# Chunk bounds from a second load of k, q turned in 32x32 blocks: a chunk-selecting attention with a gated FFN on one core

## The chip, the core and the metric

The kernel runs on one core of a Trainium2 chip. The core has TensorE for products (PE in the profile; its weight loads are listed as PEld), VectorE (DVE), ScalarE (ACT), GpSimd (POOL) and SyncE (SP), which here only issues transfers. TensorE writes to PSUM, eight banks; all else is kept in SBUF, 128 partitions wide. The metric is the device time of one execution in microseconds (us).

## The reference

```
def _attn_ref(q, k, v) -> np.ndarray:
    B, H, S, D = q.shape
    chunk = 32
    nc = S // chunk
    top_k = 6
    ...
    k_min = np.min(k_chunks, axis=3)
    k_max = np.max(k_chunks, axis=3)
    ub = np.sum(np.maximum(q[:, :, :, None, :] * k_min[:, :, None, :, :], q[:, :, :, None, :] * k_max[:, :, None, :, :]), axis=-1)
    ...
    ub = np.where(causal, ub, -1000000000.0)
    top_chunks = np.argsort(ub, axis=-1)[..., -top_k:]
    scores = scale * np.matmul(q, k.transpose(0, 1, 3, 2))
    ...
    scores = np.where(mask, scores, -1000000000.0)
    ...
    return np.matmul(attn, v).astype(np.float32)

def _moe_ref(x, w_gate, w_val, w_out, rms_g) -> np.ndarray:
    rms = np.sqrt(np.mean(x * x, axis=-1, keepdims=True) + 1e-06)
    xn = x / rms * rms_g
    g = xn @ w_gate
    silu = g * (1.0 / (1.0 + np.exp(-g)))
    val = xn @ w_val
    return (silu * val @ w_out).astype(np.float32)
```

q, k and v are fp32: batch 4, 8 heads, 768 tokens, 64 channels; the FFN has 3072 tokens, 512 wide, 1536 hidden. The mask holds the chosen chunks and causality, and attn is the softmax of the scores. Attention is causal, and a query attends only to the six chunks of 32 keys whose upper bound `ub` is highest. The result, with the heads side by side, goes through an RMS norm and a gated FFN.

## The kernel before

Work is cut into 16 pairs: a pair is two heads of one batch, and four pairs make a batch. Every piece of work is a step, recorded by `add(name, engines, ...)` with what it depends on and which buffers it opens. The long string `PROGRAM` holds the order: each word names an engine (P, A, D, G for POOL, S), the number of a step and the buffer slots that it opens. `Order.run` emits the steps in that order, and each engine runs its own steps strictly in it. A step waits for those it depends on and for the last users of its slots. The numbers in the `add` calls are what the search for an order was told; nothing in the kernel reads them at run time. `SLOTS` (line 232) says how many buffers of a kind there are.

For a pair, `prep` (line 479) loads q and k as tiles `qnat` and `knat` of 128 tokens by 2 x 64 channels, and TensorE turns each in six fp32 transposes (`turn`, line 514, tiles `pq` and `pk`). ACT or DVE evict them to `qt` and `kt`, channels on partitions (helper `evict`, lines 289 to 295, whose lines stand in the profile for many steps). From `kt`, two reductions per pair give the largest and smallest key of each chunk (`kmx`, and `ku` for the smallest, lines 546 and 548), and `dif` subtracts them. Since max(q x min, q x max) = q x min + relu(q) x (max - min), the bound is a sum of two products: `ku` with `qt`, and the difference with `rt`, which is relu of `qt` (`relu`, line 630). POOL casts `kt` to bf16 halves `ke` (`cast`, line 614), beside which `ke` holds a constant indicator of chunks, `e_all`.

For pairs from number 3 on (`QM`), q reaches its bf16 form `qs` on another way: POOL lays `qnat` out as bf16 in `qn` (`lay`, line 551), the chosen chunks are written beside it (`pick`, line 657), and SP issues two DMA transposes (`turned`, line 555) into `qs`. The same way for k is in the code for pairs from `KSIDE` on, which is 16, so that no pair takes it. For pairs from 6 on (`DUO`), two pairs share one step of bound products (`duo`, line 770): 16 products on tiles of 64 rows by 32 columns with 384 columns each, two evictions to `ubd`, six transposes back (`up`), the causal mask (`ubm`), then eight-largest searches (`top`, line 644) and `pick`, which also writes a guard row from the largest bound.

`scores` (line 843) multiplies `ke` by `qs` into `sc`, ACT takes the exponential into `pt`, POOL masks the diagonal (pairs of batch 1 on), and TensorE multiplies by `vx` into `av`. DVE normalizes into `xb`. `norm` and `ffn` (lines 937, 1017) run per batch and half: gate and val products of four matmuls each (`gp`, `vp`), tanh on ACT, `tg` and `hh` on DVE, each of which frees the PSUM bank of its product, then three times three output steps (`po`). The FFN of one batch is interleaved with the attention of the next ones. The lowest part of the program, until the first gate product of batch 0, has fillers for TensorE (`busy`, line 338).

Of the kernel before, what the change touches and what calls it, by code (L numbers as in the profile page):

```python
# [198 lines left out]
def kernel(  # L199
# [25 lines left out]
    W = S // 2  # L225
    G = 3
    DUO = 6
    KSIDE, QM = 16, 3
    HW = NT * P + D
    NPAIRS = B * NP  # L230

# [247 lines left out]
    def prep(c, i0, nb, at, lr):  # L479
# [85 lines left out]
        if side_k:  # L565
            def red2(e, which, j0, bank):
                a0, a1 = j0 * 4, (j0 + 3) * 4
                if which == 0 and mx.tile is None:
                    tile_of(mx, [P, NCH], FP32, "kmx")
# [580 lines left out]
```

## Time and profile before

| | us |
|---|---|
| median of 3 runs | 314.37 (314.15 to 315.52) |
| the profiled execution | 314.75 |
| its span, first to last instruction | 313.0 |
| busy in the span: PE, DVE, ACT, POOL | 303.2, 231.5, 185.5, 103.9 |

The profile shows one execution. A row of a group has the line, engine and operation, what it writes and reads, the count, the total busy time, the mean of one in ns, and the idle time of its engine just before it. A chain row has the start, the length and the group. Busy times contain an instruction's latency, which overlaps with the next one's start: 96 of the 128x128 transposes of k last 277 ns each and yet take less than half of that on the chain when they follow each other.

### The profile page before, as it was taken

What the parts mean: (1) busy time and instruction counts of PE and PEld (TensorE: products, weight loads), DVE (VectorE), ACT (ScalarE), POOL (GpSimd) and SP (SyncE); (2) the same over time, 40 slices, a digit from 0 to 9 for tenths busy, and PEclk for the clock granted to TensorE, in tenths of its full rate; (3) what the DMA queues carried; (4) which work ended last, traced back from release to release, by engine and by line L of the source; (5) the groups of instructions that cost most, each with busy time, mean ns of one, the idle gap of its engine ahead of it and who ended that gap; (6) DMA issues with size and microseconds to landing.
All of it is one profiled execution on the core that took longest, in us unless ns stands there. A gap on an engine that the chain in (4) does not pass through costs nothing.

```text
span 313.0 us, 7431 instructions
## 1 busy us (share of the span) xinstructions
PE 303.2 (97%) x2772; PEld 191.7 (61%) x2790; DVE 231.5 (74%) x654; ACT 185.5 (59%) x415; POOL 103.9 (33%) x162
## 2 busy tenths in 40 slices
PE   7998999999999999999999999999999999999994
PEld 3676776576576855667687546656666545555541
DVE  4998989969985789856978879989544564577551
ACT  1688998783298773697794643366697403442001
POOL 8686453371354843252377100033233110000000
PEclk9999999999999999999999999999999999999998
DMA  9999999999699996797684060361240034100014
GB/s 173 220 190 126 96 191 206 201 165 168 129 185 198 220 114 146 175 191 138 138 68 28 17 140 13 52 77 36 58 79 36 2 78 155 69 3 0 2 67 169
DMA packets 113301, 35.35 MB, mean 113 GB/s; under 512 B 106225, under 2 KB 110065, under 8 KB 113265
## 3 DMA queue, kind: packets, MB, share of 16 engines
q1 hardware_dynamic: 83152, 26.62, 41.1%
q0 software_dynamic: 28512, 7.87, 24.9%
q10 hardware_dynamic: 1600, 0.39, 0.6%
q8 instruction: 22, 0.36, 0.5%
q14 instruction: 15, 0.11, 0.1%
HBM read 28.57 MB, written 6.29 MB: 111 GB/s over the span
## 4 chain that ended last, share of the span: by engine, by line
PE 87%; DMA 5%; DVE 4%; POOL 1%; issue 1%; SPq 1%; ACT 1%; POOLq 0%
PE po L1078 20%; PE vp L1058 19%; PE gp L1037 19%; PE sc L868 9%; PE av L904 5%; DMA wv<-in_moe_w_val_dram 4%; PE pk L517 3%; PE busy L338 3%; PE pq L517 3%; PE ub L781 2%; PE ub L723 2%; PE up L803 1%; DMA qs<-qn 1%; DVE m L650 1%; DVE qs L293 1%
## 5 line engine op out<-in xcount | busy, mean ns | idle before, releaser
L885 ACT ACTIVATE pt<-sc 128x512 bf16<-128x512 f32 (+2 forms) x192 | 92.9, 561 | 17.5 <-PE sc L868 15.4
L1044 ACT ACTIVATE sg<-gp 128x384 bf16<-128x384 f32 x96 | 45.5, 496 | 55.1 <-PE gp L1037 42.2
L1050 DVE SCALAR_TENSOR_TENSOR tg<-sg,gp 128x384 bf16<-128x384 bf16 x96 | 51.8, 550 | 32.0 <-ACT sg L1044 30.6
L1058 PE MATMUL vp<-xT,wv 128*128 128x384 bf16 x384 | 74.0, 326 | 0.3 <-DMA wv<-in_moe_w_val_dram 0.2
L1037 PE MATMUL gp<-xT,wg 128*128 128x384 bf16 x384 | 73.2, 326 | 0.7 <-ACT xT L289 0.4
L1078 PE MATMUL po<-wo,hh 128*128 128x512 bf16 x272 | 66.9, 379 | 0.9 <-issue 0.2
L1066 DVE TENSOR_TENSOR hh<-vp,tg 128x384 bf16<-128x384 f32 x96 | 51.6, 552 | 12.6 <-PE vp L1058 11.7
L868 PE MATMUL sc<-qs,ke 128*128 128x128 bf16 (+5 forms) x420 | 57.1, 251 | 0.3 <-DMA qs<-qn 0.2
L1058 PEld LDWEIGHTS <-wv 128*128 128x128 bf16 x384 | 35.9, 98 | 25.0 <-issue 1.2
L1037 PEld LDWEIGHTS <-wg 128*128 128x128 bf16 x384 | 36.2, 98 | 23.9 <-issue 1.5
L1078 PEld LDWEIGHTS <-hh 128*128 128x128 bf16 x288 | 27.3, 98 | 29.1 <-issue 1.5
L904 PEld LDWEIGHTS <-pt 128*128 128x128 bf16 x672 | 35.1, 98 | 10.5 <-ACT pt L885 0.6
L904 PE MATMUL av<-vx,pt 128*128 128x65 bf16 x672 | 41.4, 193 | 0.1
L891 POOL TENSOR_SCALAR_AFFINE_SELECT pt<-pt 128x512 bf16<-128x512 bf16 (+1 forms) x48 | 24.4, 521 | 47.4 <-ACT pt L885 43.6
L868 PEld LDWEIGHTS <-ke 128*128 128x128 bf16 (+1 forms) x420 | 30.6, 97 | 9.6 <-issue 1.6
L293 POOL CAST ke<-kt 64x768 bf16<-64x768 f32 x32 | 26.6, 835 | 16.6 <-ACT kt L289 6.0
L293 POOL CAST qn<-qnat 128x768 bf16<-128x768 f32 x13 | 10.7, 822 | 40.5 <-DMA qs<-qn 40.5
L291 ACT ACTIVATE osb<-po 128x512 f32<-128x512 f32 x12 | 7.1, 599 | 24.7 <-PE po L1078 24.7
L981 DVE SCALAR_TENSOR_TENSOR xs<-xb,ri,gains 128x512 bf16<-128x512 bf16 x24 | 17.5, 751 | 2.1 <-POOL ri L973 1.7
L925 DVE TENSOR_TENSOR xb<-av,rden 128x384 bf16<-128x384 f32 (+1 forms) x34 | 18.2, 534 | 1.2
L473 POOL DMA_DIRECT2D vx<-in_v_dram x16 | 16.9, 1055 | 0.1
L650 DVE MAX8 m<-ubm 128x8 f32<-128x8 f32 (+4 forms) x192 | 16.7, 160 | 0.2
(83 smaller groups left out, 297.7 us busy)
## 6 DMA issues: line engine op xcount, KB each, us to landing
out_dram<-osb SPq DMA_DIRECT2D x24, 256.0 KB, 2.3
knat<-in_k_dram SPq DMA_DIRECT2D x30, 192.0 KB, 4.3
qnat<-in_q_dram SPq DMA_DIRECT2D x30, 192.0 KB, 4.6
vx<-in_v_dram POOLq DMA_DIRECT2D x16, 192.0 KB, 5.5
wg<-in_moe_w_gate_dram POOLq DMA_DIRECT2D x2, 768.0 KB, 11.6
wv<-in_moe_w_val_dram POOLq DMA_DIRECT2D x2, 768.0 KB, 10.0
wo<-in_moe_w_out_dram POOLq DMA_DIRECT2D x2, 768.0 KB, 10.1
qs<-qn SPq DMA_TRANSPOSE x26, 2.8
```

The lines of the kernel that those rows point to most:

```text
L293: engine[e].tensor_copy(out_, in_)
L650: nc.vector.max(out=m8.tile[:, y[0], y[1], :], in_=ubm.tile[:, y[0], y[1], 0:max(8, 4 * (i0 + x) + 4)])
L868: nc.tensor.matmul(t[:, x:x + m, :].rearrange("p a b -> p (a b)"), ke[kk, kb * P:(kb + 1) * P], qs[kk, q0 * P:(q0 + m) * P], start=not tri ...
L885: nc.scalar.activation(out=t[:, 0:nn, :], in_=sc.tile[:, 0:nn, :], func=ACT.Exp, scale=SCALE)
L891: nc.gpsimd.affine_select(out=pt.tile[:, 0:nd, :], in_=pt.tile[:, 0:nd, :], compare_op=ALU.is_ge, fill=0.0, base=0, pattern=[[0, nd], [1, ...
L904: nc.tensor.matmul(av.tile[:, qi - i0, :], pt.tile[:, x, :], VX[c.v.slot][:, hl * NT + kb, :], start=(begin and m == 0), stop=(left[0] == ...
L1037: nc.tensor.matmul(t[:], wg[:, g, hs], XT[b].tile[:, g, cols], start=(g == 0), stop=(g == NP - 1))
L1044: nc.scalar.activation(out=t[:], in_=gp.tile[:], func=ACT.Tanh, scale=0.5)
L1050: nc.vector.scalar_tensor_tensor(out=t[:], in0=sg.tile[:], scalar=1.0, in1=gp.tile[:], op0=ALU.add, op1=ALU.mult)
L1058: nc.tensor.matmul(t[:], wv[:, g, hs], XT[b].tile[:, g, cols], start=(g == 0), stop=(g == NP - 1))
L1066: nc.vector.tensor_tensor(out=t[:], in0=vp.tile[:], in1=tg.tile[:], op=ALU.mult)
L1078: nc.tensor.matmul(po.tile[:], hhs[ht].tile[:, th * P:(th + 1) * P], wo[:, ht, :], start=(ht == 0), stop=(ht == NHT - 1))
```

## The change

Pairs 6 to 15 no longer turn k and q on TensorE. Six parts:

- `bounds_of`, once for two pairs: k of four heads is loaded a second time, 96 chunks on partitions and each chunk's 32 x 64 numbers along them, in three parts of 11, 11 and 10 tokens (`kc`). DVE takes minimum and maximum over the tokens of a part (`kp`) and joins the parts (`kj`). The minimum and the difference are spread to 4 x 32 columns (`mm`), turned by four fp32 transposes (`kcT`) and evicted to `kux`.
- q for the bounds: DVE transposes `qnat` in 32x32 blocks (`qb`), and relu of it may run on POOL too.
- `duo`: with q in blocks of 32 channels, a product covers 32 rows: 64 products on 32x32 tiles with 192 columns, four evictions.
- k in bf16 goes the way of q: `KSIDE` is 6, POOL or DVE lays it out in `kb`, two DMA transposes turn it into `ke`. `kb` carries the chunk indicator, which is turned once (`et`).
- the guard row of `pick` becomes a step of its own (`grd`) for ACT, POOL or DVE.
- buffers: `nat` 6 for 7, `hh` 26 for 31, `row`, `xs` and `ob` one less each; `selq` and the fillers' zeros lie in `kb`. `PROGRAM` is another string throughout.

```
-    KSIDE, QM = 16, 3
+    KSIDE, QM, TK = 6, 3, (0, 11, 22, 32)
-    SLOTS = dict(ps=8, nat=7, kb=0, qn=2, vext=4, set=3, ku=4, selq=2, qt=7, ubs=1, ubd=1, small=8, ubm=3,
-                 pt=10, xb=2, xt=2, row=3, xs=4, ff=8, hh=31, ob=3)
+    SLOTS = dict(ps=8, nat=6, kb=2, kp=1, kj=1, mm=1, kux=2, qn=2, vext=4, set=3, ku=4, selq=2, qt=7, ubs=1, ubd=1, small=8, ubm=3,
+                 pt=10, xb=2, xt=2, row=2, xs=3, ff=8, hh=26, ob=2)
...
+    KUX = [const.tile([P, 2, 2, 4, CH], FP32, name=f"kux{i}") for i in range(SLOTS["kux"])]
+    SELQ = [x[:, 0:2 * NT * D].rearrange("p (i h e) -> p i h e", h=2, e=D) for x in KB]
...
+    cap = const.tile([P, 1], FP32, name="cap")
+    c_cap = add("cap", "DVE", 0.07, -98, lambda e: nc.vector.memset(cap[:], -GUARD))
+    c_kux = [add("kux0", "", {"POOL": 0.22 + 16 * CH * 0.00085}, {"kux0": 1.0},
+                 lambda e, i=i: nc.gpsimd.memset(KUX[i][:], 0.0)) for i in range(SLOTS["kux"])]
...
+    def bounds_of(cs):
+        b, h0, rows = cs[0].b, cs[0].h0, 4 * NCH
+        at, lr = f"a{cs[1].p}", f"l{cs[0].p}"
+        kp, mm, kux = Buf("kp"), Buf("mm"), Buf("kux")
+        ends = []
+        for x in range(3):
+            kc, n = Buf("qt"), TK[x + 1] - TK[x]
+
+            def load(e, x=x, kc=kc, n=n):
+                tile_of(kc, [P, n, D], FP32, "kc")
+                nc.sync.dma_start(
+                    out=kc.tile[0:rows],
+                    in_=k[b, h0:h0 + 4].rearrange("h (c t) d -> (h c) t d", t=CH)[:, TK[x]:TK[x + 1]])
+
+            ld = add("kcl", "SP", 0.6, rank(lr, 1, "kcl", x, "step"), load, opens=[kc], load=rows * n * D * 4)
+            for m in range(2):
+                def part(e, x=x, m=m, kc=kc):
+                    if kp.tile is None:
+                        tile_of(kp, [P, 2, 3, D], FP32, "kp")
+                    nc.vector.tensor_reduce(
+                        out=kp.tile[0:rows, m, x], in_=kc.tile[0:rows].rearrange("p t d -> p d t"),
+                        axis=AXX, op=(ALU.min, ALU.max)[m])
+
+                ends.append(add("kh", "DVE", 0.07 + n * D * 0.00104, rank(at, 1, "kh", 2 * x + m, "step"), part,
+                                [ld], opens=[kp], uses=[kc]))
+
+        both = Buf("kj")
+
+        def join(e):
+            t = tile_of(both, [P, 2, D], FP32, "kj")
+            for m in range(2):
+                nc.vector.tensor_reduce(
+                    out=t[0:rows, m], in_=kp.tile[0:rows, m].rearrange("p x d -> p d x"),
+                    axis=AXX, op=(ALU.min, ALU.max)[m])
+
+        jn = add("kf", "DVE", 0.54, rank(at, 1, "kf"), join, ends, opens=[both], uses=[kp])
+
+        def spread(e):
+            t = tile_of(mm, [P, 2, 2, 4, CH], FP32, "mm")
+            lo, hi = (both.tile[0:rows, m].rearrange("p (g o e) -> p g o e", o=1, e=CH).to_broadcast(
+                [rows, 2, 4, CH]) for m in range(2))
+            engine[e].tensor_copy(t[0:rows, 0], lo)
+            engine[e].tensor_tensor(out=t[0:rows, 1], in0=hi, in1=lo, op=ALU.subtract)
+
+        sp = add("kdif", "", {"DVE": 0.55, "POOL": 0.9}, rank(at, 1, "kdif"), spread, [jn], opens=[mm], uses=[both],
+                 port=True)
+        bank = Buf("ps", "prep")
+
+        def turn(e):
+            t = tile_of(bank, [P, 2, 2, rows], FP32, "kcT")
+            for m in range(2):
+                for x in range(2):
+                    nc.tensor.transpose(t[:, m, x], mm.tile[0:rows, m, x].rearrange("p r e -> p (r e)"),
+                                        ident_f[0:rows, 0:rows])
+
+        tr = add("kcT", "PE", 4 * 0.085, rank(at, 1, "kcT"), turn, [sp, c_id], opens=[bank], uses=[mm])
+
+        def out_(e):
+            evict(e, KUX[kux.slot][:].rearrange("p m x y c -> p (m x y) c")[:, :, 0:NCH],
+                  bank.tile[:].rearrange("p m x (y c) -> p (m x y) c", c=NCH))
+
+        ev = add("kcE", "", {"ACT": act(4 * rows), "DVE": dve(4 * rows)}, rank(at, 1, "kcE"), out_, [tr] + c_kux,
+                 opens=[kux], uses=[bank])
+        for c in cs:
+            c.kux, c.kready = kux, [ev]
...
-            for j0 in range(0, nb, 3):
+            for j0 in range(0, nb, 3) if p < DUO else ():
...
-                if w == "k" and side_k:
-                    kbanks.append((j0, bank, tr))
-                    continue
...
-        df = add("dif", "", {"DVE": 0.12, "POOL": 0.2}, rank(at, b, "dif"), diff, reds,
+        df = None if side_k else add("dif", "", {"DVE": 0.12, "POOL": 0.2}, rank(at, b, "dif"), diff, reds,
...
+        if p >= DUO:
+            def turn_q(e):
+                t = tile_of(big["q"], [P, S], FP32, "qb")
+                nc.vector.transpose(out=t[:], in_=nat["q"].tile[:].rearrange("p t h d -> p (t h d)"))
+
+            done["q"] = [add("qB", "DVE", dve(S), rank(at, b, "qB"), turn_q, ready["q"][:1], opens=[big["q"]],
+                             uses=[nat["q"]])]
...
-                nc.vector.tensor_scalar(out=t[:, 0:n], in0=big["q"].tile[:, 0:n], scalar1=0.0,
+                engine[e].tensor_scalar(out=t[:, 0:n], in0=big["q"].tile[:, 0:n], scalar1=0.0,
...
+            def guard(e):
+                if side_q:
+                    s12 = QN[qn.slot][:, D:D + 2 * NT * P].rearrange("p (t d) -> p t d", d=P)
+                    m12 = m8.tile[:].rearrange("p h i e -> p (h i) e")
+                else:
+                    s12 = SELQ[sq.slot][:, 0:nb].rearrange("p i h e -> p (i h) e")
+                    m12 = m8.tile[:, 0:nb].rearrange("p i h e -> p (i h) e")
+                o, m = s12[:, :, NCH:NCH + 1], m12[:, :, 0:1]
+                if e == "ACT":
+                    nc.scalar.activation(out=o, in_=m, func=ACT.Relu, bias=cap[:, 0:1])
+                else:
+                    engine[e].tensor_scalar(out=o, in0=m, scalar1=-GUARD, scalar2=0.0,
+                                            op0=ALU.add, op1=ALU.max)
+
+            gd = add("grd", "", {"ACT": 0.22, "POOL": 0.25, "DVE": 0.12}, rank(at, b, "sel"), guard,
+                     last + (c_qn if side_q else c_sel) + [c_cap], opens=[qn if side_q else sq], uses=[m8],
+                     port=True)
...
-        n, at, b = S // 2, f"a{cs[1].p}", cs[0].b
-        ub, ubs = [Buf("ps", "prep") for _ in range(2)], Buf("ubd")
+        n, at, b = S // 4, f"a{cs[1].p}", cs[0].b
+        ub, ubs = [Buf("ps", "ub") for _ in range(4)], Buf("ubd")
 
         def bounds(e):
             t = [tile_of(x, [P, n], FP32, "ub") for x in ub]
             for m in range(2):
-                for y in range(4):
-                    c = cs[y // 2]
-                    for h in range(2):
-                        rows = slice(h * D, (h + 1) * D)
-                        nc.tensor.matmul(
-                            t[h][y * CH:(y + 1) * CH, :], KU[c.ku.slot][rows, m, :],
-                            c.bound[0][m].tile[rows, (y % 2) * n:(y % 2 + 1) * n],
-                            start=(m == 0), stop=(m == 1), tile_position=(h * D, y * CH))
-
-        um = add("ub", "PE", 0.25 + 0.8 * n / 256, rank(at, b, "ub"), bounds,
-                 [x for c in cs for x in c.bound[1]], opens=ub,
-                 uses=[x for c in cs for x in (c.ku,) + c.bound[0]])
-        ubms, done = [Buf("ubm") for _ in cs], [[], []]
-        for h in range(2):
-            def ub_out(e, h=h):
+                for dh in range(2):
+                    for y in range(4):
+                        c, h = cs[y // 2], y % 2
+                        for g in range(4):
+                            rows = slice(g * CH, (g + 1) * CH)
+                            nc.tensor.matmul(
+                                t[g][y * CH:(y + 1) * CH, :].rearrange("p (t e) -> p t e", e=CH),
+                                KUX[c.kux.slot][rows, m, dh, y, :],
+                                c.bound[0][m].tile[rows].rearrange("p (t h g e) -> p h g t e", h=2, g=2, e=CH)
+                                [:, h, dh], start=(m == 0 and dh == 0), stop=(m == 1 and dh == 1),
+                                tile_position=(g * CH, y * CH))
+
+        um = add("ub", "PE", 1.6, rank(at, b, "ub"), bounds,
+                 [x for c in cs for x in c.bound[1] + c.kready], opens=ub,
+                 uses=[x for c in cs for x in (c.kux,) + c.bound[0]])
+        ubms, done, ues = [Buf("ubm") for _ in cs], [[], []], []
+        for g in range(4):
+            def ub_out(e, g=g):
                 if ubs.tile is None:
-                    tile_of(ubs, [P, 2, n], FP32, "ubd")
-                evict(e, ubs.tile[:, h], ub[h].tile[:])
-
-            ue = add("ubE", "", {e: {"ACT": act(n), "DVE": dve(n)}[e] for e in BOUNDS},
-                     rank(at, b, "ubE", h, "step"), ub_out, [um], opens=[ubs], uses=[ub[h]])
+                    tile_of(ubs, [P, NT, 4, CH], FP32, "ubd")
+                evict(e, ubs.tile[:, :, g], ub[g].tile[:].rearrange("p (t e) -> p t e", e=CH))
+
+            ues.append(add("ubE", "", {e: {"ACT": act(n), "DVE": dve(n)}[e] for e in BOUNDS},
+                           rank(at, b, "ubE", g, "step"), ub_out, [um], opens=[ubs], uses=[ub[g]]))
+        for z in range(2):
             up = Buf("ps", "prep")
 
-            def up_turn(e, h=h, up=up):
+            def up_turn(e, z=z, up=up):
                 t = tile_of(up, [P, 3, P], FP32, "up")
                 for j in range(3):
-                    nc.tensor.transpose(t[:, j], ubs.tile[:, h, j * P:(j + 1) * P], ident_f[:])
-
-            ut = add("up", "PE", 0.33, rank(at, b, "up", h, "step"), up_turn, [ue], opens=[up], uses=[ubs])
+                    nc.tensor.transpose(t[:, j], ubs.tile[:, 3 * z + j].rearrange("p g e -> p (g e)"), ident_f[:])
+
+            ut = add("up", "PE", 0.33, rank(at, b, "up", z, "step"), up_turn, ues, opens=[up], uses=[ubs])
             for x, c in enumerate(cs):
...
+    every = [make_pair(p) for p in range(NPAIRS)]
     for p in range(NPAIRS):
-        c, b = make_pair(p), p // NP
+        c, b = every[p], p // NP
+        if p >= DUO and p % 2 == 0:
+            bounds_of(every[p:p + 2])
...
+    c_kb[0].deps += turns
```

More of the change, by code (lines that the diff above doesn't have):

```diff
@@ L309 @@
     QN = [const.tile([P, 2 * HW + P], BF16, name=f"qn{i}") for i in range(SLOTS["qn"])]
-    SELQ = [const.tile([P, NT, 2, D], BF16, name=f"selq{i}") for i in range(SLOTS["selq"])]
+    KUX = [const.tile([P, 2, 2, 4, CH], FP32, name=f"kux{i}") for i in range(SLOTS["kux"])]
+    SELQ = [x[:, 0:2 * NT * D].rearrange("p (i h e) -> p i h e", h=2, e=D) for x in KB]
+    turns = []
     VX = [const.tile([P, 2 * NT, D + 1], BF16, name=f"vx{i}") for i in range(SLOTS["vext"])]
@@ L331 @@
         out=first[:], in_=ident_f[:, 0:1], func=ACT.Exp), [c_id])
-    zeros = const.tile([P, 4 * P], BF16, name="zeros")
-    c_zero = add("zeros", "DVE", 0.2, -101, lambda e: nc.vector.memset(zeros[:], 0.0))
+    zeros = KB[0][:, 2 * HW:2 * HW + P]
+    c_zero = add("zeros", "DVE", 0.2, -101, lambda e: nc.vector.memset(zeros, 0.0))
     def busy(bank, n):
@@ L337, in go @@
             t = tile_of(bank, [P, 4 * P], FP32, "busy")
[L338 removed]
+            nc.tensor.matmul(
+                t[:, 0:n], zeros, zeros.rearrange("p (o n) -> p o n", o=1).to_broadcast([P, n // P, P]),
+                start=True, stop=True)
         return go
@@ L708, in prep @@
         if p >= DUO:
-            c.bound = (big["q"], rel), [rl] + [c.dif[x] for x in c.dif], choose
+            c.bound = (big["q"], rel), [rl], choose
             return
```

47 lines of the change are left out of this document (14 added, 33 removed), and 246 rows, old and new, of the table PROGRAM.

## The prediction

> **What bounds the kernel now.** I read the page first (busy shares, the slices, the chain), then TensorE's waits, then a table of windows cut at TensorE's first gate product of batch 0, 1 and 2 (51.2, 126.7, 184.7 us).
>
> ```profile
> PE 303.2 (97%) x2772; PEld 191.7 (61%) x2790; DVE 231.5 (74%) x654; ACT 185.5 (59%) x415; POOL 103.9 (33%) x162
> DVE  4998989969985789856978879989544564577551
> PEclk9999999999999999999999999999999999999998
> PE 87%; DMA 5%; DVE 4%; POOL 1%; issue 1%; SPq 1%; ACT 1%; POOLq 0%
> ```
> ```profile
> PE busy L338 <- DVE zeros L333: 2.2, 1, 2.2
> PE ub L723 <- DVE qs L293: 0.8, 1, 0.8
> PE gp L1037 <- ACT xT L289: 0.4, 1, 0.4
> PE vp L1058 <- DMA wv<-in_moe_w_val_dram: 0.2, 1, 0.2
> ```
> ```profile
> 0.00:51.20 51.20, 47.21 (x579) 32.98 (x582) 42.94 (x131) 38.54 (x85) 31.62 (x55) 1.00 1.13 169
> 51.20:126.70 75.50, 74.63 (x709) 48.52 (x713) 62.84 (x197) 50.52 (x116) 33.80 (x48) 1.00 1.10 171
> 126.70:184.70 58.00, 57.73 (x585) 38.20 (x587) 46.04 (x119) 43.14 (x97) 23.86 (x36) 1.00 0.67 105
> 184.70:260.90 76.20, 75.75 (x641) 45.92 (x644) 51.15 (x157) 39.56 (x88) 14.58 (x23) 1.00 0.29 57
> ```
> The window columns are length, then busy time of PE, PE's weight loads, DVE, ACT and POOL, the clock, the DMA share and GB/s. From 51 us on TensorE works without a break at full clock: 74.63 of 75.50, 57.73 of 58.00, 75.75 of 76.20, and its longest waits (2.2, 0.8, 0.4 us) are over before. So work taken off TensorE there is time saved, as long as the next engine can follow. That engine is DVE: 62.84 of 75.50 and 46.04 of 58.00, together 108.9 of 133.5 us or 82%.
>
> **What the change takes off TensorE and puts on it.** The built orders of both kernels give the counts: fp32 transposes of k and q fall from 96 and 96 to 36 and 36, that is by 120. In the old order 108 of those stand behind the first gate product; in the new one none does.
>
> ```profile
> 108.77 0.66 PE pk L517 x6
> 109.70 0.36 PE pk L517 x3
> 73.17 1.45 PE ub L781 x32
> ```
> ```profile
> 30.09 0.52 PE L747 MATMUL up<-ident_f,ubs 96*128 96x96 f32 x4
> 30.45 0.29 PE L904 MATMUL av<-vx,pt 128*128 128x65 bf16 x4
> 73.10 0.18 PEld L781 LDWEIGHTS ub<-qt,ku 64*32 64x32 f32 x16
> 105.03 0.25 PE av L904 x8
> 34.02 0.51 PE L694 MATMUL st<-ident_b,selq 128*128 128x128 bf16 x6
> 34.37 1.10 PE L904 MATMUL av<-vx,pt 128*128 128x65 bf16 x21
> ```
> On the chain six transposes cost 0.66 us, or three 0.36 where they stand alone: 120 are 13.2 to 14.4 us, and I take 13.5 off. Added: 20 transposes of 96 rows (`kcT`). The nearest rows are four of 96 partitions which begin at 30.09, with the next product at 30.45: 0.09 each, 1.8 us. The indicator's six bf16 transposes (`et`) cost what the six at 34.02 did until 34.37: 0.35 us.
>
> The bound products (`ub`) change shape: per duo 16 products on tiles of 64x32 with 384 columns become 64 on tiles of 32x32 with 192. The trace has each as two records, 32 in 1.45 us. Columns per tile stay the same (four records of 384 before, eight of 192 after), so 1.45 us is the low bound if sixteen tiles run side by side as eight do. If the bound is the rate at which instructions start, the closest row is 16 weight loads within 0.18 us, 11 ns each: 128 pairs of load and product would need 1.4 us. The far bound is a pair that does not share the array, 8 products in 0.25 us or 31 ns: 128 of them, 4.0 us. I take 1.6, close to the row of the same operation: +0.75 us for five duos, with 0 and +12.8 as ends.
>
> The Trainium skill ("TensorE: Matmul & The Clock Gate", Back-to-back issue gap and Part 1) says that start-to-start never drops below about 25 ns however few columns there are. By that rule 128 records would be 3.2 us and the five duos +8.75 us. The row speaks against it for tiles, since sixteen loads start in 0.18 us. The same page's part on packing has tiles 4 ns apart.
>
> TensorE's sum: -13.5 + 1.8 + 0.35 + 0.75 = -10.6 us.
>
> **What it puts on DVE.**
>
> ```profile
> L546 DVE TENSOR_REDUCE kmx<-kt 128x24 f32<-128x768 f32 (+1 forms) x17 | 15.3, 897 | 1.5 <-ACT kt L289 1.5
> L548 DVE TENSOR_REDUCE ku<-kt 128x24 f32<-128x768 f32 (+1 forms) x17 | 15.1, 893 | 0.0
> L293 DVE COPY qt<-pq 128x384 f32<-128x384 f32 x9 | 4.9, 551 | 1.8 <-PE pq L517 1.8
> L635 DVE TENSOR_SCALAR rt<-qt 128x768 f32<-128x768 f32 x4 | 2.2, 552 | 0.1
> L668 DVE TENSOR_SCALAR qn<-m 128x12 bf16<-128x12 f32 x13 | 2.9, 225 | 0.0
> L665 DVE SCALAR_TENSOR_TENSOR qn<-m,ubm 128x288 bf16<-128x288 f32 x13 | 5.9, 451 | 0.1
> L674 DVE SCALAR_TENSOR_TENSOR selq<-m,ubm 128x288 bf16<-128x288 f32 x3 | 2.7, 899 | 0.1
> L810 DVE TENSOR_TENSOR ubm<-up,cmf 128x144 f32<-128x144 f32 x20 | 5.6, 301 | 1.5 <-PE up L803 1.2
> L293 DVE COPY ubs<-ub 96x256 f32<-96x256 f32 x4 | 1.7, 415 | 0.7 <-PE ub L723 0.7
> ```
> Between the first gate products of batch 0 and 2 the old order has 20 reductions (20 x 0.895 = 17.9 us), 11 copies of transposed halves (6.1), three `rt` (1.7) and eight small guards (1.8) that the new one does without: -27.5. It adds 28 of the 30 reductions of `kc` into `kp`. By the rows above, 704 elements at the rate of 768 in 0.897 are 0.82 us and 640 are 0.75, so 22.3 us. Ten 32x32 block transposes of q, 768 elements: no row has one; the bounds are `rt` at 0.552 and `kmx` at 0.897. I take 0.88, the one-element-a-cycle row, 8.8 us. Ten joins of 192 elements lie between 144 in 0.301 and 256 in 0.415: 3.4. Nine more bound copies of 192: 3.2. The spread (two steps of two instructions), one `kux` and one bf16 layout of k: about 2.5. Together +40.2, net +12.7.
>
> DVE would then hold 108.9 + 12.7 = 121.6 us in a stretch that TensorE's loss shortens from 133.5 to about 123. That is the crux: the cover behind which these instructions are free, 18% idle time, is nearly used up. Where DVE is late, gate and val products wait next, for their PSUM banks are freed by `tg` and `hh` on DVE. The old rows show no stall at 83%; at 97 to 99% I price the queueing at 3.5 us, an estimate: about a quarter of the net addition does not find a gap in time. Its bounds are 0 (DVE's busy rows overlap by some 0.08 us an instruction, as 0.897 against the 0.86 by which reductions follow each other on the chain at 22 us) and 12.7 (none finds one).
>
> ```profile
> 21.74 0.83 DVE ku L548
> 22.58 0.86 DVE kmx L546
> ```
> **What lies on other engines.** ACT loses 27 evictions of `kt` and `qt` and five `rt`, and gains small copies and guards: off the path. POOL trades 21 half casts of k for nine whole ones and nine `rt`, about even, with 23.86 of 58 us busy. The transfers:
>
> ```profile
> L293 POOL CAST qn<-qnat 128x768 bf16<-128x768 f32 x13 | 10.7, 822 | 40.5 <-DMA qs<-qn 40.5
> qs<-qn SPq DMA_TRANSPOSE x26, 2.8
> knat<-in_k_dram SPq DMA_DIRECT2D x30, 192.0 KB, 4.3
> 83.01 6.73 SPq L557 DMA_TRANSPOSE qs<-qn  x4
> 79.13 2.55 SPq L557 DMA_TRANSPOSE qs<-qn  x2
> 81.73 1.17 SPq L497 DMA_DIRECT2D knat<-in_k_dram  x2
> ```
> SP issues 20 more transposes at 1.28 us (2.55 for two) and 15 more loads at 0.59, 34 us in all. It is densest between the first gate products of batch 1 and 2, where the new order has 30 transposes and 35 plain transfers, 38 + 21 = 59 us.
>
> ```profile
> 100.12 0.65 PE gp L1037 x4
> 100.77 0.86 PE po L1078 x4
> ```
> That stretch was 58.00 us and now holds eight more gate and val steps and nine more output parts, 58 + 8 x 0.65 + 9 x 0.86 = 71 us before the transposes leave (45 x 0.11 = 5) and moved scores come, so about 70. A transpose waits on SP for its bf16 layout, and the loads behind it in the queue wait along. If they come late, the scores that need `ke` are late next. I cost this at nothing, since pairs are loaded and turned ahead of their scores in the order. Without that cover one transpose costs its 2.8 us of landing plus its issue, 4 us, and I let it happen at most twice.
>
> Ahead of the first gate product twelve transposes leave and nine score products of pair 4 come forward with their exponentials; I set this stage to zero, with 1.5 us either way.
>
> **The sum.** Against the profiled execution (314.75 us, of which the span is 313.0, and 1.75 lies around it): 314.75 - 10.6 + 3.5 = 307.65. The median of the runs is 314.37, 0.38 less, which gives 307.3 us.
>
> **The rivals.** *Strided reads at half rate (slower than before).* Each `kp` reduction walks along t with d outside, so neighbouring elements lie 64 x 4 = 256 bytes apart, while `kmx` and `ku` read consecutive ones. No row of this trace has such a read. That one instruction can take twice as long under other conditions is seen at lines 665 and 674: the same operation on 128x288 at 451 and 899 ns. At double price the 28 reductions cost 22.3 us more, DVE holds 144 us, and TensorE waits in a stretch of which it fills 123: +21 us in place of my 3.5, so 314.37 - 10.6 + 21 = 324.8. The 0.08 us overlaps in busy time and DVE's room before and behind (51.15 of 76.20) can take up to some 8 us of this: 317 to 325, say 320. It turns slower than before when a reduction takes over 0.82 + (10.6 - 3.5)/28 = 1.07 us. For it: the pattern. Against: a reduction moves one element a cycle already, the slowest rate of the trace, and does not depend on packing. The Trainium skill has rules for either side. "SBUF — State Buffer" (Door 1, on cachelines) says that accesses which cross to a new 16-byte line each time pay a penalty, so fp32 can step four elements freely. "VectorE: DVE Perf Modes" (Mode 1x) calls that mode the fallback which takes odd strides as they come. The trace shows neither. Chance 0.27.
>
> *Everything hides.* The order keeps DVE's chain ahead, and the loss is 0 to 1: 303.8 to 304.8. For it: no wait of TensorE over 0.4 us behind 51 us today. Against: DVE at over 97%. Chance 0.14.
>
> *The transfers come late.* Two or three pairs whose `ke` lands after their scores could start, 4 us each in place of gains: 311 to 315. Against: SP still has 11 of some 70 us free there, and DMA moves only 105 GB/s in the window from 126.7 us, against 171 in the one before. Chance 0.14.
>
> *The bounds do not pack.* At 4.0 us a duo TensorE gains 12 us less than I count, but then DVE has room and the 3.5 fall away: 303.8 + 12 = 315.8; midway 310. Chance 0.08, as the trace's tiles start 11 ns apart.
>
> **Chances and range.** The forecast (304.8 to 311, likeliest 307.3) has the remaining 0.37. A kernel of these spreads is told apart from no change at about 0.5%, here 312.8 and 315.9. Faster: 0.37 + 0.14 + 0.08 of the late transfers + 0.05 of the bounds = 0.64. Same: 0.06 + 0.02 = 0.08. Slower: 0.27 + 0.01 = 0.28. The range runs from 302.8, the full gain and a microsecond from the first stage, to 321; left out are about 0.05 below and 0.13 above. The forecast's own range is 304.8 to 311.
>
> **What will show it.** `kp<-kc` at about 0.8 us (right) or 1.5 (the first rival). `qb<-qnat` at about 0.9. The chain's pieces of 128 `ub` records at 1.6 us, or 3 to 4. DVE's busy time between the first gate products of batch 0 and 2 over 95%, with TensorE waits on `tg` or `hh` of some 3.5 us in all; none of these would make the loss wrong. TensorE waits on `ke` would show late transfers. The prediction is wrong in kind if TensorE's idle time behind the first gate product exceeds 10 us.

## The result and the profile after

| | before | after |
|---|---|---|
| median, us | 314.94 (314.15 to 316.4, 4 runs) | 324.2 (322.62 to 324.9, 4 runs) |
| span of the profiled execution | 313.0 | 322.3 |
| TensorE busy / idle in the span | 303.2 / 9.8 | 301.0 / 21.3 |

The ratio is 1.0282 (95% interval 1.0225 to 1.0338): slower by 2.8%. The forecast was 307.3 us, and its range ended at 321. The mechanism of the main rival, strided reads, came true, but at another price and as one of four causes. Some executions of any of these kernels take a few per cent longer than the rest; times and ratios here leave those out, and of the profiles below only that of `e3_both` is of such an execution.

TensorE's busy time fell by 2.2 us where the sum had 10.6, and its idle time grew by 11.5 us where the sum had 3.5. So about half of the miss lies in TensorE's busy time and half in its waiting.

From the page of the kernel after: busy shares, the slices of DVE and of the DMA engines, and the shares of the chain.

```profile
PE 301.0 (93%) x3173; PEld 184.8 (57%) x3173; DVE 250.1 (78%) x664; ACT 181.9 (56%) x404; POOL 117.2 (36%) x163
DVE  2989879999799799899698898867468968366610
DMA  9999999999989998999995999996300222020013
PE 53%; DVE 17%; DMA 9%; ACT 7%; POOL 6%; issue 4%; SPq 3%; POOLq 0%; DVEq 0%; ACTq 0%
```

TensorE was 87% of the chain before and is 53% now. DVE, DMA and POOL hold 17, 9 and 6% (4, 5 and 1% before): no single new bound, but several, each of which ends waits somewhere. The DMA engines read 9 in 24 of the first 28 slices. In the kernel before they read 9 in the first ten, and less than that in 13 of the next 18:

```profile
DMA  9999999999699996797684060361240034100014
```

The windows, cut at the first gate product of batch 0, 1, 2 and 3 (columns as in the prediction):

```profile
0.00:56.68 56.68, 49.19 (x594) 32.76 (x595) 44.31 (x150) 43.90 (x97) 39.09 (x58) 1.00 1.23 173
56.68:127.63 70.95, 66.68 (x813) 41.46 (x813) 66.26 (x165) 42.23 (x98) 31.55 (x44) 1.00 1.20 169
127.63:212.29 84.66, 78.97 (x1032) 49.62 (x1032) 74.28 (x220) 51.05 (x114) 38.11 (x49) 1.00 1.07 169
212.29:259.45 47.16, 46.99 (x412) 29.39 (x411) 33.50 (x73) 29.28 (x66) 8.39 (x14) 1.00 0.37 70
```

The first stage is 5.5 us longer (56.7 for 51.2). Between the first gate products of batch 0 and 2 TensorE is idle for 4.27 + 5.69 = 10.0 of 155.6 us, where the old order lost 1.1 of 133.5. Behind that it is busy as before: the loss lies where the changed work is. DVE holds 66.26 + 74.28 = 140.5 us of that stretch, 90%. The clock is 1.00 in every window, so it is no cause.

The groups that the change touches:

```profile
L506 DVE TENSOR_REDUCE kp<-kc 96x64 f32<-96x704 f32 (+1 forms) x30 | 39.4, 1327 | 1.5 <-DMA kc<-in_k_dram 1.3
L697 POOL TENSOR_SCALAR rt<-qb 128x768 f32<-128x768 f32 x5 | 10.7, 2138 | 8.3 <-DVE qb L687 8.3
L697 POOL TENSOR_SCALAR rt<-qt 128x768 f32<-128x768 f32 x4 | 8.8, 2199 | 0.2
L687 DVE STREAM_TRANSPOSE qb<-qnat 128x768 f32<-128x768 f32 x10 | 9.7, 971 | 0.6 <-DMA qnat<-in_q_dram 0.6
L856 PE MATMUL ub<-rt,kux 32*32 32x192 f32 x320 | 7.9, 331 | 1.3 <-issue 1.3
L518 DVE TENSOR_REDUCE kj<-kp 96x64 f32<-96x192 f32 x10 | 3.1, 353 | 0.0
```

Against the prices of the prediction: the reductions took 1.33 us for 0.8, POOL's relu 2.14 to 2.20 for the 0.82 of a cast, the block transposes 0.97 for 0.88, the joins 0.35 for 0.34. The chain shows where three of them end up, with the bound products of a duo as one piece:

```profile
8.08 2.14 POOL rt L697
26.32 2.13 POOL rt L697
43.05 6.96 DMA qs<-qn
60.03 1.27 DVE kp L506
98.55 5.64 DMA qs<-qn
111.87 2.50 DVE kp L506 x2
198.06 2.32 PE ub L856 x109
```

And the transfers (KB and median us from issue to landing in the last columns):

```profile
q1 hardware_dynamic: 100832, 34.49, 58.3%
kc<-in_k_dram SPq DMA_DIRECT2D x10, 264.0 KB, 4.4
qs<-qn SPq DMA_TRANSPOSE x26, 4.1
ke<-kb SPq DMA_TRANSPOSE x20, 4.4
```

The queue of SP's transfers took 41.1% of the engines' time before and 58.3% now, and the transposes of q, which were there already, land after 4.1 us in place of 2.8. On the chain one takes 7 us.

### The profile page after: what moved, and what is told of

The parts are those of the page before. It is cut to its first block, busy times and chain, and to the rows that moved or that the text cites. A ratio compares the mean times of both kernels' runs of the same rounds, so it can differ in the third digit from the quotient of the medians.

```text
span 322.3 us, 8261 instructions
## 1 busy us (share of the span) xinstructions
PE 301.0 (93%) x3173; PEld 184.8 (57%) x3173; DVE 250.1 (78%) x664; ACT 181.9 (56%) x404; POOL 117.2 (36%) x163
## 2 busy tenths in 40 slices
DMA packets 130983, 43.27 MB, mean 134 GB/s; under 512 B 122464, under 2 KB 126304, under 8 KB 130944
## 3 DMA queue, kind: packets, MB, share of 16 engines
q1 hardware_dynamic: 100832, 34.49, 58.3%
## 4 chain that ended last, share of the span: by engine, by line
PE 53%; DVE 17%; DMA 9%; ACT 7%; POOL 6%; issue 4%; SPq 3%; POOLq 0%; DVEq 0%; ACTq 0%
PE po L1156 14%; PE vp L1136 13%; PE gp L1115 12%; DVE kp L506 5%; DMA qs<-qn 5%; PE sc L946 5%; ACT pt L963 4%; PE av L982 3%; SPq L627 3%; POOL rt L697 3%; DMA kc<-in_k_dram 2%; DVE tg L1128 2%; PE ub L856 2%; DVE hh L1144 2%; DMA knat<-in_k_dram 1%
## 5 line engine op out<-in xcount | busy, mean ns | idle before, releaser
L1122 ACT ACTIVATE sg<-gp 128x384 bf16<-128x384 f32 x96 | 44.7, 494 | 58.9 <-PE gp L1115 54.6
L1156 PE MATMUL po<-wo,hh 128*128 128x512 bf16 x288 | 69.5, 379 | 0.0
L1128 DVE SCALAR_TENSOR_TENSOR tg<-sg,gp 128x384 bf16<-128x384 bf16 x96 | 51.0, 547 | 15.0 <-ACT sg L1122 13.8
L969 POOL TENSOR_SCALAR_AFFINE_SELECT pt<-pt 128x256 bf16<-128x256 bf16 (+1 forms) x48 | 25.0, 528 | 55.5 <-ACT pt L963 55.4
L506 DVE TENSOR_REDUCE kp<-kc 96x64 f32<-96x704 f32 (+1 forms) x30 | 39.4, 1327 | 1.5 <-DMA kc<-in_k_dram 1.3
L982 PE MATMUL av<-vx,pt 128*128 128x65 bf16 x672 | 38.0, 193 | 1.7 <-POOL pt L969 1.2
L982 PEld LDWEIGHTS <-pt 128*128 128x128 bf16 x672 | 32.3, 98 | 11.0 <-issue 1.3
L291 ACT ACTIVATE osb<-po 128x512 f32<-128x512 f32 x16 | 9.6, 600 | 23.1 <-PE po L1156 20.0
L1051 POOL TENSOR_TENSOR ri<-ms,mhalf 128x3 f32<-128x3 f32 x8 | 7.0, 876 | 40.2 <-DVE ms L1043 40.2
```

The lines of the kernel that those rows point to most:

```text
L506: nc.vector.tensor_reduce(out=kp.tile[0:rows, m, x], in_=kc.tile[0:rows].rearrange("p t d -> p d t"), axis=AXX, op=(ALU.min, ALU.max)[m])
L969: nc.gpsimd.affine_select(out=pt.tile[:, 0:nd, :], in_=pt.tile[:, 0:nd, :], compare_op=ALU.is_ge, fill=0.0, base=0, pattern=[[0, nd], [1, ...
L982: nc.tensor.matmul(av.tile[:, qi - i0, :], pt.tile[:, x, :], VX[c.v.slot][:, hl * NT + kb, :], start=(begin and m == 0), stop=(left[0] == ...
L1122: nc.scalar.activation(out=t[:], in_=gp.tile[:], func=ACT.Tanh, scale=0.5)
L1128: nc.vector.scalar_tensor_tensor(out=t[:], in0=sg.tile[:], scalar=1.0, in1=gp.tile[:], op0=ALU.add, op1=ALU.mult)
L1156: nc.tensor.matmul(po.tile[:], hhs[ht].tile[:, th * P:(th + 1) * P], wo[:, ht, :], start=(ht == 0), stop=(ht == NHT - 1))
```

## The experiments

Each time stands beside runs of the kernel before on the same chip, whose medians lay between 314.7 and 315.0. A ratio is that to the kernel before, with its 95% interval. An edit "on the double edit" stands on top of the first two together.

### The two dear instructions

`e1_pool_copy`: POOL copies q into `rt` where it took relu (nine pairs), so those bounds are not the reference's.

```
-    engine[e].tensor_scalar(out=t[:, 0:n], in0=big["q"].tile[:, 0:n], scalar1=0.0, ...)
+    nc.gpsimd.tensor_copy(t[:, 0:n], big["q"].tile[:, 0:n])      # on POOL
```

> The nine relu steps that POOL has become plain copies on POOL (the bounds are then those of q against q, not of q against relu(q): part of the computation is changed). All else is the changed kernel. POOL theory: relu on POOL takes 2.14 to 2.20 us in the trace and a cast of the same 128x768 numbers 0.83; four of them stand ahead of the first gate product (56.7 us against 51.2 before), the chain of waits holds 2.6% of POOL relu, so the first gate product falls to 51 to 53 us and the whole to 314 to 317. Reduction theory: the loss is DVE's, the first gate product moves 3 us at most, the time stays at 320 to 323.

`e2_kp_flat`: the reductions read consecutive numbers, 64 groups of 11, which are not the tokens of a channel.

```
-    in_=kc.tile[0:rows].rearrange("p t d -> p d t")
+    in_=kc.tile[0:rows].rearrange("p t d -> p (t d)").rearrange("p (d t) -> p d t", d=D)
```

> The 30 partial reductions read the same 704 or 640 numbers in the order in which they lie, so the bounds are of other groups of numbers (part of the computation is changed). All else is the changed kernel. Reduction theory: the mean falls from 1.33 to 0.80 us if the step of 256 bytes is the cause, DVE is freed of 15 us of which the stages behind the first gate product lost 16, and the whole falls to 310 to 314. If it stays at 1.33 the cause is the form with 64 outputs of 11, not the step. POOL theory: the mean may fall, but the whole stays at 320 to 323.

`e3_both` is the double edit.

> Both edits together (POOL copies in place of relu, reductions that read consecutive numbers; part of the computation is changed). If these two prices are all that the sum missed beside the bound products (2.5 us a duo in place of 1.6, 4.5 us in all), the whole comes to 307.3 + 4.5 less what hides: 306 to 312. If it stays above 316, a third cause is larger than both, and the landing of transposes (4.1 and 4.4 us against 2.8 before) is the first suspect.

Groups of the double edit:

```profile
L506 DVE TENSOR_REDUCE kp<-kc 96x64 f32<-96x704 f32 (+1 forms) x30 | 25.0, 847 | 1.4 <-DMA kc<-in_k_dram 1.4
L697 POOL COPY rt<-qb 128x768 f32<-128x768 f32 x5 | 4.1, 828 | 9.2 <-DVE qb L687 9.1
```

Both prices fall to what the prediction had (0.85 and 0.83). The time goes from 324.2 to 319.3 us without POOL's relu (ratio 1.0144, 1.0101 to 1.0188), to 316.6 without the strides (1.0042, 0.9978 to 1.0107), and to 315.7 without either (1.0009, 0.9963 to 1.0055). That is 4.9, 7.6 and 8.5 us; the two hide each other in part. Each of the three lies between the ranges that were expected for its theories: both prices count, and neither is all. Together they are half of the 16.9 us between forecast and result, so there were other causes. The first gate product came at 55.1 us with POOL's copies and not at 51 to 53, so POOL's relu is the smaller part of what the first stage lost.

`e4_relu_moved` leaves nothing out: the same nine relus on DVE (pairs 0 to 4) and on ACT, as in the kernel before, which had none on POOL.

> The nine relu steps of POOL go to other engines at the same places of the order, the four of pairs 0 to 4 to DVE and the five later ones to ACT; all is computed. POOL theory: DVE takes 0.47 us for one, ACT 0.86, so the time is that of the run with copies or 1 to 2 us above it, 314 to 318. Reduction theory: DVE gets 1.9 us more, 321 to 325.

It took 321.4 us (1.0216, 1.0159 to 1.0273), 2.8 less than the changed kernel. The two intervals overlap, and the time lies in the range of the reduction theory: moving the relu gains little, if anything. A cheap copy on POOL was worth 4.9; here the work is still there, on average 0.79 us on DVE (0.54 to 1.22, where 0.47 was expected) and 0.85 on ACT.

### What makes a strided read dear

`e5_pad65` lays the tokens of `kc` 65 numbers apart, on top of `e4_relu_moved`.

```
-    tile_of(kc, [P, n, D], FP32, "kc")
+    tile_of(kc, [P, n, 65], FP32, "kc")      # loads and reductions use [:, :, 0:D]
```

> The nine relus from POOL on DVE and ACT (321.4 us) and the second loads of k laid down with 65 numbers to a token in place of 64, so the reductions step 260 bytes; all of the computation is there. If the dear step comes from a power of two (the same place of the memory met again and again), kp falls from 1.33 to 0.85 us as with consecutive numbers. If it comes from every step that leaves a short neighbourhood, kp stays at 1.3. The loads now land in pieces of 256 bytes: if packets are what weighs, they land later than 4.4 us and the time goes above 321.4; else, with kp cheap, 315 to 317.

```profile
L506 DVE TENSOR_REDUCE kp<-kc 96x64 f32<-96x704 f32 (+1 forms) x30 | 41.1, 1384 | 2.4 <-DMA kc<-in_k_dram 2.4
```

A step of 260 bytes is as dear as one of 256. The loads, now in 144,903 packets all told in place of 130,983, landed after 5.0 and 4.5 us (4.4 and 4.0 before the edit). The time was 324.0 us (1.027, 1.0216 to 1.0323), not clearly above the 321.4 before the edit.

`e15_steps` reads the same 704 numbers in other orders, in 20 of the 30 reductions, each step on its own line.

```
+    w = kc.tile[0:rows].rearrange("p t d -> p (t d)").rearrange("p (a t s) -> p a s t", s=step, t=n)
+    nc.vector.tensor_reduce(out=o, in_=w, axis=AXX, op=op)      # step 1, 2, 4, 8, 16, 32, 64
```

> The changed kernel, in which 20 of the 30 reductions (the ones of 704 elements) read the same 704 numbers in another order, with steps of 1, 2, 4, 8, 16, 32 or 64 numbers between neighbours (4 to 256 bytes), each step on a line of its own; the bounds are not k's but for step 64. Known: step 1 takes 0.85 us and step 64 1.33 to 1.4. Theory (each read that leaves a line of 16 bytes pays): 0.85 for 1, about 0.85 to 0.95 for 2, full price from 4 on: 1.3 to 1.4 for 4, 8, 16, 32 and 64. Rival (the price grows with the distance, or comes at one far step alone): 4 and 8 stay under 1.0 and only 32 or 64 reach 1.3.

Lines 515, 517, 519, 521, 523, 525 and 527 are steps of 1, 2, 4, 8, 16, 32 and 64 numbers:

```profile
L519 DVE TENSOR_REDUCE kp<-kc 96x64 f32<-96x704 f32 x4 | 5.7, 1426 | 0.0
L521 DVE TENSOR_REDUCE kp<-kc 96x64 f32<-96x704 f32 x4 | 5.7, 1426 | 0.0
L523 DVE TENSOR_REDUCE kp<-kc 96x64 f32<-96x704 f32 x4 | 5.4, 1350 | 0.0
L527 DVE TENSOR_REDUCE kp<-kc 96x64 f32<-96x704 f32 x2 | 2.7, 1352 | 0.8 <-DMA kc<-in_k_dram 0.8
L525 DVE TENSOR_REDUCE kp<-kc 96x64 f32<-96x704 f32 x2 | 2.7, 1326 | 0.0
L517 DVE TENSOR_REDUCE kp<-kc 96x64 f32<-96x704 f32 x2 | 1.7, 872 | 0.0
L515 DVE TENSOR_REDUCE kp<-kc 96x64 f32<-96x704 f32 x2 | 1.7, 855 | 0.0
```

The price has one cliff, between a step of 2 and one of 4 numbers: 0.86 and 0.87 us, then 1.33 to 1.43 without any growth with distance. So neighbours 8 bytes apart are as good as free, and neighbours 16 bytes apart cost all of it; a step of 12 bytes was not run. The Trainium skill ("SBUF — State Buffer", Door 1) has 16-byte lines, asks for two hits a line and names four fp32 as the free step; the first two agree with these rows, the third does not, since a step of four costs all of it. This run took 324.8 us (a single execution).

### What else takes time: transposes, loads, bound products

`e7_both_nokx`: the double edit without the 20 DMA transposes of k (`turned` returns for `kX`; the scores of pairs 6 to 15 read an earlier pair's `ke`).

> The kernel with cheap reductions and a plain POOL copy for rt (315.8 us, the double edit), and beside that without the 20 transposes that lay k out by DMA (the scores of those pairs read an earlier pair's k). Theory: what the two prices leave over, some 8 to 10 us above the forecast, is partly the transposes' landing, 4.3 us against 2.8 before, which TensorE meets as 7.6 us of waits for qs in the double edit's trace: without these 20 the landing of qs falls to 3 us or less and the time to 310 to 313 us. Rival (the extra loads of k fill the DMA engines, the transposes only suffer): landing stays near 4 us and the time at 314.5 to 316. Second rival (nothing of DMA, the rest is TensorE's own work): 315 to 316 and landing shorter.

313.6 us (0.994, 0.9904 to 0.9977), 2.2 less. `qs` still landed after 3.9 us, though TensorE waited for it less:

```profile
PE sc L950 <- DMA qs<-qn: 1.5, 1, 1.5
```

The two runs below that keep both transposes and loads (`e9_both_halfub`, `e11_both_halfcols`) have 4.0 and 2.8 us there. The transposes of k are a small part, and without them the others land no sooner: as the main cause the first suspect was wrong.

`e8_both_noload`: the double edit without the 15 second loads of k.

```
-    in_=kc.tile[0:rows]...
+    in_=gains[0:rows, 0:D].rearrange("p (d o) -> p d o", o=1).to_broadcast([rows, D, n])
```

> The double edit (315.8 us) without the 15 loads of k by chunks; the reductions read 64 numbers of another tile again and again instead, so the bounds are not k's. Theory of the transposes: the loads weigh little, 314.5 to 316 us. Rival (4 MB more through the DMA engines, in packets of under 512 bytes, set the landing of everything): qs lands in 3 us or less and the time falls to 310 to 313 us.

`e12_both_tinyload` keeps the 15 issues on SP and cuts what they carry to 4 bytes.

> The double edit (315.8 us) in which the 15 second loads of k are issued as before but carry 4 bytes each instead of 240 or 264 KB; the reductions read 64 numbers of another tile again and again, so the bounds are not k's. Without the loads altogether the time was 310.6. Theory (their bytes on the DMA engines delay everything else that lands): 310 to 311.5, first gate product at 52 to 53 us. Rival (their issues on SP delay the transposes and loads queued behind them): 314.5 to 316.

310.6 us without the loads (0.9848, 0.9797 to 0.99) and 309.6 with empty ones (0.9834, 0.9781 to 0.9887), 5.1 and 6.1 us less: it is their bytes, not their place in SP's queue. Both edits also spare DVE 1.3 us of reductions (0.80 us each in place of 0.85) and 1.4 us of waiting for these loads, so up to 2.7 us of the gain need not come from what the bytes do to other transfers. TensorE's waits for q's transposes, with the loads (the double edit with fewer bound products, below) and with empty ones (us in total, times, longest):

```profile
PE sc L948 <- DMA qs<-qn: 4.0, 4, 1.8
```
```profile
PE sc L947 <- DMA qs<-qn: 0.9, 2, 0.6
```

The first gate product starts at 53.1 to 55.0 us in three profiles on the double edit that keep the loads, and at 52.5 to 53.3 in the three without: about 1.5 of the 5 to 6 us come back before the FFN begins.

`e9_both_halfub`: the double edit with half of the bound products (`for m in range(1)`: those of the difference of the bounds are left out).

> The double edit (315.8 us) with half of the bound products of a duo: 32 of 64, those with the difference of the bounds are left out. A duo's products took 2.3 to 2.5 us in the traces. Theory (instructions start 16.7 ns a pair of load and product once the queue filled ahead is used up): the half takes 0.8 to 1.0 us a duo, since the first 32 pairs start 6.7 ns apart, then as long as the last ones take to end; five duos save about 7 us at most, and the time falls to 309 to 311 if nothing else is late. Rival (columns set the pace): half of 2.4, 1.2 us, 6 us saved, 310. Second rival (TensorE isn't what ends the stretch, DMA is): the row shrinks and the time stays above 313.5.

`e11_both_halfcols`: all 64 products, but 48 of them over 96 of their 192 columns.

```
+    tt = NT if m + dh == 0 else NT // 2
...
+    ..., [:, h, dh, 0:tt], start=(m == 0 and dh == 0), stop=(m == 1 and dh == 1), ...
```

> The double edit (315.8 us) with all 64 bound products of a duo, of which 48 go over 96 of their 192 columns (three of every four; the other half of their columns is left out of the bounds). A duo's 128 records take 2.25 us undisturbed. Theory (instructions start 16.7 ns apart once those filled ahead are used up, whatever their columns): still 2.1 to 2.25 us a duo and the time at 315 to 316.5. Rival (columns set the pace): five eighths, 1.4 us a duo, and 4 us less, 311 to 312.

The chain's piece of one duo: the changed kernel, half the products, fewer columns.

```profile
81.82 2.29 PE ub L856 x111
```
```profile
78.62 1.21 PE ub L858 x59
```
```profile
80.09 1.81 PE ub L859 x97
```

Half of the products took 1.21 us and the time fell to 309.9 us (0.9816, 0.9747 to 0.9885), 5.9 less. With fewer columns a duo took 1.81 us, between both theories (2.1 or more, 1.4), and the time was 313.4 (0.9967, 0.9936 to 0.9998), between both again. Neither starts nor columns alone set the pace; a sum of both costs fits. A tile gets 1536 columns in 128 records of the whole, 768 in 64 of the half, 960 in 128 of the last. 576 columns less save 0.48 us, 0.83 ns each; then 64 records cost 1.08 - 768 x 0.83 = 0.44 us, 6.9 ns each, with 0.13 us left over. Three points fix three numbers, so the only test is the old shape: 32 records and 1536 columns a tile give 1.63 us, and its row had 1.45. So the sum is an estimate to some 12%, and that costs add is not shown beyond this fit. In the changed kernel two of the five duos were also broken up by gaps in which the profile names nothing that they waited for, and took 2.6 and 3.7 us.

`e13_halfub` makes the same cut in the changed kernel itself.

> The changed kernel (324.2 us) with half of the bound products of a duo left out and nothing else edited, so kp and rt stay dear. If TensorE's own work is felt in full even where DVE and POOL are late, the 6 us that it saved in the double edit come off here too: 317.5 to 319. If DVE and POOL set the end of the stretch, TensorE only waits longer for them: 322 to 324.5.

318.8 us (1.0136, 1.0076 to 1.0195): 5.4 come off, where the first expectation had 317.5 to 319 and the second 322 or more. What TensorE saves is felt nearly in full even where DVE and POOL are late. The interval is 3.7 us wide, so some part of it may still turn into waiting.

`e10_all` sets everything aside: no DMA transposes of k, no second loads, half of the bound products.

> The double edit (315.8 us) with all three: no DMA transposes of k, no second loads of k, half of the bound products. If the three causes make up what is left, the forecast's working holds for the rest: 314.4 - 13.5 + 1.8 + 0.4 for the transposes on TensorE and less some 2 to 4 us for the halved products is 299 to 302 us. If a cause is still missing (the stage ahead of the first gate product, moved scores), it stays above 305.

305.1 us (0.9679, 0.963 to 0.9728). One at a time the three gave 2.2 + 5.1 + 5.9 = 13.2, together 10.6. It is above the 299 to 302 expected and just over the 305 that was to mean a missing cause; the first gate product is at 53.3 us, still 2.1 behind, and that is left unexplained. The bound products took 5 x 1.21 = 6.05 us here, for which the prediction had 8.0: on its prices this kernel would stand at 307.1, beside a forecast of 307.3 that held 3.5 for queueing. The span splits into 291.9 us in which TensorE is busy and 11.5 in which it is idle. With 8.0 us of bound products it would be busy for 293.9, where the sum had 303.2 - 10.6 = 292.6, and the sum's idle time was 9.8 + 3.5 = 13.3. So the sum closes to about 2 us in either part. Between the first gate products of batch 0 and 2 TensorE loses 2.8 us here, with DVE as busy (126.35 of 140.08 us, 90%) as in the changed kernel:

```profile
53.28:193.36 140.08, 137.33 (x1525) 86.53 (x1524) 126.35 (x383) 93.21 (x214) 62.35 (x92) 1.00 0.97 142
```

### A kernel with all of it

`e14_oneload` leaves nothing out. k of a pair is turned in 32x32 blocks by DVE and reduced over consecutive numbers; only pairs 12 and 13 are loaded twice; four products a duo (`kcT<-kj,rep`) spread the bounds; the relus are moved as in `e4_relu_moved`. Fifteen words of `PROGRAM` were moved by hand.

```
+    nc.vector.transpose(out=t[:], in_=nat.tile[:].rearrange("p t h d -> p (t h d)"))
...
+    nc.vector.tensor_reduce(out=kp.tile[:, m, i], in_=kcs[x].tile[:].rearrange("p (c t) -> p c t", t=CH), ...)
...
+    nc.tensor.matmul(t[:, g], REP[:, g].rearrange("p o e -> p (o e)"),
+                     both.tile[:].rearrange("p m y t -> p (m y t)"), start=True, stop=True)
```

> A kernel that computes all of it and leaves out the three dear parts of the change: the chunk bounds of k no longer come from a second load (eight of the ten pairs; pairs 12 and 13 still load their k twice), but from the pair's own k, turned in 32x32 blocks by DVE like q, with two reductions over consecutive numbers a pair (0.97 + 2 x 0.9 us, against 4.4 us a pair in the changed kernel); four products of 128 rows a duo spread the bounds over the partition groups; the nine relus on POOL are on DVE and ACT. If the causes found make up the loss (second loads 5.2 us, strided reductions about 7, the relu about 3, of which some overlap: 8 to 10 together from 324.2, and 5 from the loads), it takes 308 to 312 us, less than the kernel before (314.8). Rival (the order was searched for the other prices, and k's earlier loads and the moved steps cost as much as they save): 313 to 318.

No execution took less than 325.0 us (ratio 1.0481, 1.0432 to 1.0529): worse than both and above the rival's range too. The profile of the fastest:

```profile
L511 DVE TENSOR_REDUCE kp<-kc 128x24 f32<-128x768 f32 x20 | 18.0, 942 | 0.1
L556 PE MATMUL kcT<-kj,rep 128*128 128x96 f32 x40 | 5.3, 275 | 0.0
```
```profile
DVE qb L705 <- DMA qnat<-in_q_dram: 4.6, 3, 2.1
```
```profile
PE sc L964 <- DVE hh L1162: 3.5, 2, 1.7
```

The reductions cost what was planned (0.94 us), but the spreading products kept TensorE busy for 5.3 us (2.9 for the transposes in their place before), and DVE now stands still for loads of q, perhaps pushed back by the earlier loads of k. The scores wait for DVE. The hand-moved order is part of this run, so it doesn't say what such a kernel would take in an order searched for it; that stays open.

## Why the prediction was wrong, point by point

- *DVE's reductions (step "I take 0.82 and 0.75").* The failed term that weighs most: 1.33 us, past the 1.07 us that the prediction itself named as the turning point. The rival had the place and the sign right and the size wrong (some 1.6 times as long, not twice), and that its time of 320 was near the result is partly luck: strides alone are worth 7.6 us, where its 320 stands 12.7 above the forecast. Its evidence "against", that a reduction moves one element a cycle anyway, did not hold: reading can be slower than that.
- *POOL ("about even").* The relu was in effect given the price of a cast, without a row for it. It took 2.14 to 2.20 us, 1.3 more each, 4.9 us of the time. The pieces on the chain at 8, 26, 75 and 182 us show why POOL's low share (36%) didn't protect: q's bounds wait for that very instruction.
- *Transfers ("at nothing").* The step looked at SP's queue and at 105 GB/s in one window. The runs put the cost elsewhere: 3.9 MB more on engines whose slices already read 9 through the first quarter of the old span cost 5 to 6 us (up to 2.7 of it perhaps through DVE), about 1.5 of them in the first stage, which was set to zero with 1.5 either way and lost 5.5. The transposes of k add some 2 us. The rival of late transfers named `ke`; it was `qs`, which landed late.
- *Bound products (+0.75).* Measured 2.25 to 2.3 us a duo undisturbed in place of 1.6, and the five, with two broken up, took 13.2 us from their first records to the next product, where the old row makes 7.3 of five. The working took the larger of two limits, 1.45 for columns and 1.4 for starts; the runs fit a sum. The Trainium skill ("TensorE: Matmul & The Clock Gate", Back-to-back issue gap) has start to start never below some 25 ns, which gives 3.2 us; 2.29 us for 128 records is 17.9 ns each, so for tiles side by side the trace goes against it, as the prediction said.
- *Transposes off TensorE (-13.5).* Not tested alone. With the causes above set aside TensorE's busy time comes to within 1.3 us of the working (293.9 for 292.6); that this term is right is argued from that sum, not shown.
- *Queueing (3.5).* DVE's load without the excess of the strides is 140.5 - 28 x 0.53 = 125.7 us, where 121.6 was foreseen. The 97 to 99% was set against a stretch of 123 us, which leaves out the gate, val and output products that the working itself moves in later (58 to about 70 us), and the `tg` and `hh` that come with them (44.5 us of DVE before, 49.5 after). The stretch lasted 155.6 us with DVE busy for 90%, so the sign of over 95% did not come, and TensorE's waits there for `tg` and `hh` are 2.2 of its 10.0 us idle, not 3.5. TensorE's idle time behind the first gate product is 21.3 - 7.5 = 13.8 us, past the 10 that the prediction called wrong in kind (9.8 - 4.0 = 5.8 before).

## What to carry to other kernels

An instruction whose access pattern or engine has no row in the trace must be bounded by more than the row of the same operation: a step of 16 bytes or more made this reduction 1.6 times as long, and another ALU operation made POOL 2.6 times as long as a copy. Look at the share of time that the DMA engines are busy, not at GB/s or at the issuing queue: here they read 9, and further bytes cost time. Work taken off the bounding engine is worth its time only if all that replaces it stays within what the other engines have free; here DVE's reductions, POOL's relu, the second loads and the bound products did not.

## What the runs showed of the hardware

- Reductions of 704 fp32 on DVE: 0.86 to 0.87 us with a step of 1 or 2 numbers, 1.33 to 1.43 with any step of 4 to 64 numbers.
- POOL: 128x768 fp32, copy 0.83 to 0.87 us, maximum with a constant 2.14 to 2.20.
- Products on sixteen 32x32 tiles of TensorE: 2.29 us for 128 records with 1536 columns a tile, 1.21 for half of them; a fit of three shapes gives 6.9 ns a record plus 0.83 ns a column.
- DMA transposes landed after 2.8 us beside a queue at 41%, 4.1 to 4.4 at 58%, and 3.4 for q's without the second loads.
